# Attention followed by a mixer: the negated maxima reach their matrix row by a DMA instead of a masked multiplication

## The chip, the cores and the metric

The kernel runs on one core of a Trainium2 chip. A core has five engines that run in parallel, each through its own list of instructions in a fixed order: TensorE (PE; its weight loads are listed as PEld), VectorE (DVE), ScalarE (ACT), GpSimd (POOL) and SyncE (SP), which here issues all the DMAs. They wait for each other on semaphores. The metric is the device time of one execution in microseconds (us), lower is better; the number compared is the median of several runs.

## What is computed

```python
def _attn_ref(q, k, v):                     # 8 batches x 8 heads, 576 rows, 64 columns, float32
    scores = scale * np.matmul(q, k.transpose(0, 1, 3, 2))
    mask = block_i >= block_j               # blocks of 64 rows: causal by block
    scores = np.where(mask, scores, -1000000000.0)
    scores = scores - np.max(scores, axis=-1, keepdims=True)
    attn = np.exp(scores)
    attn = attn / (np.sum(attn, axis=-1, keepdims=True) + 1e-09)
    return np.matmul(attn, v)

def _moe_ref(x, U, V, w_ch1, w_ch2):        # x: the heads side by side, 8 x 576 x 512
    h = x.transpose(0, 2, 1) @ U @ V        # mixing over the rows, rank 32
    u = x + h.transpose(0, 2, 1)
    return u + np.maximum(u @ w_ch1, 0.0) @ w_ch2     # 512 -> 2048 -> 512
```

## The kernel before

There are 64 heads. For one head the work runs through these steps, each a function of the kernel that adds tasks to a list:

- `split_qk` fetches q and k (transposed, 64 x 1152) into `raw`, rounds them into `qa` and `kk`, and puts what the rounding lost into `qb` and the second half of `kk`. Two DMAs (`qb<-qa`, `kk<-kk`) copy rounded parts into other partitions. The subtractions that give the lost parts can run on POOL or on DVE.
- `maxima` multiplies queries by keys on PE (lines L1255 and L1257), takes the negated maximum of each row of scores on DVE (L1264, into five columns of `mx`), transposes these columns on PE (L1272) and copies the resulting 5 x 128 block to `mr` on ACT or DVE (L1276, L1277). Then `spread` (L1281, POOL or DVE) multiplies this block by `sel`, a 5 x 640 mask of ones and zeros, and writes 5 x 640 elements into rows 96 to 100 of `qa`. In each column only one of the five rows is not zero. The five rows of `kk` that meet them in the next product are ones, so that product adds the negated maximum of a query to all its scores.
- `probabilities` multiplies keys by queries (L1303 with `qa`, L1304 with `qb`), this time with the maxima in, and takes the exponential on ACT (L1317 for heads 0 to 7, L1325 after them) with a scale of 0.125 and, as a bias read from the tile `lift`, 8 ln 2. From head 8 on the result is split in two float16 parts `pp` (L1328 on ACT, L1333 on DVE).
- `apply_v` multiplies by the values (L1353, L1357 to L1359); `mix` does, after every second head, the mixing over rows (L1402, L1416, L1419).

Eight heads make a batch. When the eight are done, the feed-forward network can work on that batch, in chunks of 288 rows: `ffn_chunk` (first product L657, second L682) for the first half of the 2048 hidden columns. When all heads are done, `block_products` (L899) does the second half.

The order of all of this is not the order of the code. A planner, class `Plan`, keeps a table of tasks with an engine (or several to choose from), an estimated time, a priority (1000 x head for attention, from a million up for the feed-forward products) and dependencies. It plays these through, and whenever an engine is free in the plan it issues the ready task with the lowest priority number. Constants say when each engine starts (`START`), how long a result takes to be seen by another engine (`TAIL`, `INTO`), and how long a DMA lasts (`after=DL`, 3000 ns). PSUM banks come from pools: four in `banks_a` (of which `Rest` leaves one alone), one double bank in `banks_w`, two for the feed-forward in `banks_f`. In the plan's first 260 us, when PE has nothing to do, it issues a pair of matmuls of zeros (`idle`, L1503), counted as 225 ns.

Of the kernel before, what the change touches and what calls it, by code (L numbers as in the profile page):

```python
# [28 lines left out]
SCALE = 0.125  # L29
# [66 lines left out]
class Part:  # L96
# [8 lines left out]
    def __bool__(self):  # L105
        return bool(self._free())

    def pop(self, _):
        return self.pool.pop(self._free()[0])

    def append(self, x):
        self.pool.append(x)


class Rest:
# [175 lines left out]
def attention_then_mixer(  # L291
# [10 lines left out]
    nc = tc.nc  # L302
# [10 lines left out]
    def f32(ap):  # L313
        return ap.bitcast(F32)
# [734 lines left out]
    mx_r = [b.split(5) for b in ring(ap, 2, [P, P], F32, "mx")]  # L1049
    mr_r = ring(ap, 2, [P, P], F32, "mr")  # L1050
    sel = buf(ap, [P, 5, P], F32, "sel")
    vr_r = ring(ap, 2, [P, 10, D], F32, "vr")
# [22 lines left out]
    for n, fill in enumerate((1.0, NEG)):  # L1075
# [6 lines left out]
    make_identity(nc, ident.ap)  # L1082
    nc.gpsimd.memset(sel[96:P], 0.0)
    nc.gpsimd.affine_select(
        out=sel[96:P], in_=sel[96:P], pattern=[[-1, 5], [0, P]], compare_op=ALU.not_equal, fill=1.0, base=0,
        channel_multiplier=1,
    )
    nc.vector.memset(f32(qa_r[0][0:64, 0:64]), 0.0)
# [146 lines left out]
    def maxima(h, pr):  # L1235

        qa, kk, mx, mr = qa_r[h % NB], kk_r[h % NB], mx_r[h % 2], mr_r[h % 2]
        for tiles in ((4, 0), (3,), (2, 1)):
            wide = tiles[0] == 4
            bank = Buf(pool=banks_w if wide else Rest(banks_a))  # L1240
            parts, at = [], 0
            for i in tiles:
                n = P * i + 64
# [17 lines left out]
            for i, view in parts:  # L1261
# [6 lines left out]
                )  # L1268
        bank = Buf(pool=banks_a)
        rows = slice(96, 101)  # L1270
# [4 lines left out]
        add(  # L1275
            "ACT", _act(P), pr + 2, lambda: nc.scalar.copy(mr[rows], bank[rows, 0:P]), [bank], [mr],  # L1276
            others=[("DVE", _dve(P), lambda: nc.vector.tensor_copy(mr[rows], bank[rows, 0:P]), False, 50)],  # L1277
        )

        def spread(e):  # L1280
            return lambda: e.tensor_tensor(  # L1281
                out=qa[rows, :].rearrange("p (i c) -> p i c", i=5), in0=mr[rows].unsqueeze(1).to_broadcast([5, 5, P]),
                in1=sel[rows], op=ALU.mult,
            )

        add(
            "POOL", 1340, pr + 2, spread(nc.gpsimd), [mr], [qa.parts[1]], others=[("DVE", _dve(W), spread(nc.vector), True, 500)],
        )

    def probabilities(h, pr):  # L1290
# [5 lines left out]
        for g, (a, b, tiles) in enumerate(GROUPS):  # L1296
            bank = Buf(pool=Rest(banks_a) if g else banks_w)

# [11 lines left out]
            def shaped(x, g=g):  # L1310
                return x if g else x.rearrange("p (j k) -> p j k", j=2)

            view = lambda g=g, bank=bank, n=b - a: bank[:, :n] if g else bank[:, :, :320]
            if h < FW:
                add(
                    "ACT", _act(b - a) + 90, pr,
                    lambda view=view, at=at, shaped=shaped: nc.scalar.activation(  # L1317
                        shaped(pw_r[h % 2][:, at]), view(), AF.Exp, bias=lift[:, 0:1], scale=SCALE
                    ),
                    [bank], [ph.parts[g], pl.parts[g]],  # L1320
                )
                continue
            add(
                "ACT", _act(b - a) + 90, pr,
                lambda view=view: nc.scalar.activation(view(), view(), AF.Exp, bias=lift[:, 0:1], scale=SCALE), [], [bank],  # L1325
            )
# [10 lines left out]
    def apply_v(h, pr):  # L1337
# [40 lines left out]
    def mix(p, pr):  # L1378
# [166 lines left out]
```

## Time and profile before

| | us |
|---|---|
| median of three runs | 1136.38 |
| the three runs | 1133.79, 1136.38, 1136.84 |
| the profiled execution, whole | 1133.6 |
| its span, first to last instruction | 1131.5 |
| PE busy in the span | 1104.0 |
| DVE busy in the span | 973.8 |
| ACT busy in the span | 673.9 |
| POOL busy in the span | 443.7 |

The profile is of one execution. An engine is busy while one of its compute instructions runs. Idle time is listed with the instruction that followed it and with the engine whose result ended it. PE's matmuls of zeros count as busy although they compute nothing. Attention takes the part of the span up to about 630 us, with feed-forward products mixed in from batch to batch; what follows is feed-forward alone.

### The profile page before, as it was taken

Reading aid. Unit: us, or ns where it says so; the run is one execution under the profiler, and the core shown is the slowest. Engines: PE = TensorE matmul, PEld = TensorE weight load, DVE = VectorE, ACT = ScalarE, POOL = GpSimd, SP = SyncE. Lnnn points to the kernel's source line nnn. Section 1 sums busy time; section 2 is a strip of 40 time slices with the busy share of each in tenths; the row PEclk is TensorE's granted clock in tenths of the full one; section 3 lists DMA queues with packets and bytes.
Section 4 is the critical chain, followed back from the end, with each engine's and each line's share of the span. In section 5 each row is a group of like instructions: output and inputs, shape, how many; then the busy total and the mean of one; then the engine's idle time right before and its main releaser. Section 6 shows DMA issues by size and latency. Waiting matters only on the chain.

```text
span 1131.5 us, 27523 instructions
## 1 busy us (share of the span) xinstructions
PE 1104.0 (98%) x10722; PEld 921.2 (81%) x10722; DVE 973.8 (86%) x1983; ACT 673.9 (60%) x1294; POOL 443.7 (39%) x451
## 2 busy tenths in 40 slices
PE   9999998999999999999999999999999999999998
PEld 8897777888888888888888877777777777777776
DVE  7899899999999999999988537322799999999998
ACT  5568696777776778767767533531445545545543
POOL 4646565646586647564635293651000000000000
PEclk9999999999999999999999999999999999999999
DMA  7754565455455445445352225131231331340321
GB/s 166 190 154 119 173 190 138 139 137 147 132 148 141 131 127 147 127 117 140 98 127 54 72 68 163 43 85 48 59 103 35 116 116 35 102 127 32 95 85 42
DMA packets 82418, 126.39 MB, mean 112 GB/s; under 512 B 14448, under 2 KB 58480, under 8 KB 82288
## 3 DMA queue, kind: packets, MB, share of 16 engines
q1 hardware_dynamic: 82288, 124.64, 39.8%
q8 instruction: 84, 1.38, 0.5%
q14 instruction: 46, 0.38, 0.1%
HBM read 76.23 MB, written 29.49 MB: 93 GB/s over the span
## 4 chain that ended last, share of the span: by engine, by line
PE 61%; DVE 28%; ACT 4%; issue 3%; DMA 2%; POOL 2%; SPq 0%; POOLq 0%; DVEq 0%; ACTq 0%
PE bb L899 29%; DVE mx L1264 7%; PE bf L682 6%; PE bf L657 6%; PE bg L657 4%; PE bg L682 4%; DVE pp L1333 4%; DMA st<-in_w_dram 2%; DVE hl L665 1%; DVE wr L379 1%; DVE z L371 1%; PE ba L1357 1%; PE ba L1358 1%; PE ba L1359 1%; DVE x L1372 1%
## 5 line engine op out<-in xcount | busy, mean ns | idle before, releaser
L682 PEld LDWEIGHTS <-w2h 128*128 128x128 f16 x1024 | 100.3, 98 | 27.9 <-issue 2.6
L657 PEld LDWEIGHTS <-w1h 128*128 128x128 f16 x1024 | 97.7, 98 | 27.4 <-issue 3.0
L899 PE MATMUL bb<-hh,w1h 128*128 128x288 f16 x448 | 118.9, 286 | 0.0
L899 PE MATMUL bb<-hh,w1l 128*128 128x288 f16 x448 | 118.9, 286 | 0.0
L899 PE MATMUL bb<-hh,w2h 128*128 128x288 f16 x448 | 118.9, 286 | 0.0
L899 PE MATMUL bb<-hh,w2l 128*128 128x288 f16 x448 | 118.9, 286 | 0.0
L682 PE MATMUL bf<-hh,w2h 128*128 128x288 f16 x384 | 110.5, 288 | 2.4 <-DVE hl L665 2.4
L682 PE MATMUL bf<-hl,w2h 128*128 128x288 f16 x384 | 109.8, 286 | 0.0
L682 PE MATMUL bf<-hh,w2l 128*128 128x288 f16 x384 | 109.8, 286 | 0.0
L899 PEld LDWEIGHTS <-w1h 128*128 128x128 f16 x896 | 87.7, 98 | 21.9
L899 PEld LDWEIGHTS <-w2h 128*128 128x128 f16 x896 | 87.7, 98 | 21.9
L827 ACT CAST hh<-hb 128x576 f16<-128x576 f32 x96 | 63.8, 666 | 68.4 <-DVE hb L853 45.8
L899 PE MATMUL bb<-hl,w1h 128*128 128x288 f16 x448 | 91.6, 286 | 0.0
L899 PE MATMUL bb<-hl,w2h 128*128 128x288 f16 x448 | 91.6, 286 | 0.0
L1169 POOL TENSOR_TENSOR qb<-raw,qa 64x576 fp32r<-64x576 f32 x50 | 70.9, 1418 | 48.5 <-ACT pp L1328 9.3
L1357 PE MATMUL ba<-vv,pp 128*128 128x65 f16 x840 | 88.0, 194 | 0.3
L1358 PE MATMUL ba<-vv,pp 128*128 128x64 f16 x840 | 87.7, 195 | 0.0
L1359 PE MATMUL ba<-vv,pp 128*128 128x65 f16 x840 | 87.0, 192 | 0.2 <-DVE pp L1333 0.2
L1264 DVE TENSOR_REDUCE mx<-ba 128x1 f32<-128x448 f32 (+2 forms) x192 | 85.8, 476 | 0.9 <-ACT wr L483 0.6
L1281 POOL TENSOR_TENSOR qa<-mr,sel 5x640 fp32r<-5x640 f32 x44 | 67.8, 1541 | 40.1 <-ACT mr L1276 15.5
L1357 PEld LDWEIGHTS <-pp 128*128 128x128 f16 x840 | 77.8, 96 | 2.8 <-issue 0.9
L1358 PEld LDWEIGHTS <-pp 128*128 128x128 f16 x840 | 78.3, 97 | 1.7 <-issue 0.4
(227 smaller groups left out, 3459.5 us busy)
## 6 DMA issues: line engine op xcount, KB each, us to landing
raw<-in_qk_dram SPq DMA_DIRECT2D x63, 288.0 KB, 3.8
st<-in_w_dram SPq DMA_DIRECT2D x32, 512.0 KB, 4.3
o_d<-ot SPq DMA_DIRECT2D x72, 144.0 KB, 1.8
qb<-qa SPq DMA_DIRECT2D x64, 144.0 KB, 2.8
kk<-kk SPq DMA_DIRECT2D x64, 144.0 KB, 3.1
ur<-u_d SPq DMA_DIRECT2D x64, 144.0 KB, 2.7
wr<-o_d SPq DMA_DIRECT2D x32, 288.0 KB, 3.2
vr<-in_v_dram SPq DMA_DIRECT2D x28, 320.0 KB, 3.2
```

Source lines behind the costliest of these rows:

```text
L371: return nc.vector.scalar_tensor_tensor(out=z, in0=upp, scalar=-(1 << 30), in1=z, op0=ALU.bitwise_and, op1=ALU.bitwise_or)
L657: nc.tensor.matmul(ps[:, :T], w()[wn][:, k, fs], m[k].ap, start=(i == 0), stop=(i == len(ops) - 1))
L682: nc.tensor.matmul(ps[:, :T], w()[wn][:, f, ms], hs[f][x].ap, start=(i == 0), stop=(i == len(ops) - 1))
L827: add("ACT", _act(2 * T, True), E, lambda: nc.scalar.copy(h.ap, x[0]()), [x[1]], [h])
L899: nc.tensor.matmul(bank[:, i, :T], x()[:, w(k)], p.ap[:, k, :], start=first and n == 0, stop=last and n == len(ops) - 1)
L1169: sub = lambda e, dst=dst, x=x, y=y: lambda: e.tensor_sub(dst, raw[:, x], f32(y))
L1264: lambda i=i, view=view: nc.vector.tensor_reduce(out=mx[:, 96 + i : 97 + i], in_=view(), op=ALU.max, axis=AX.XY if i == 4 else AX.X, negat ...
L1281: return lambda: e.tensor_tensor(out=qa[rows, :].rearrange("p (i c) -> p i c", i=5), in0=mr[rows].unsqueeze(1).to_broadcast([5, 5, P]), in ...
L1333: lambda at=at, view=view, shaped=shaped: nc.vector.tensor_sub(shaped(pl[:, at]), view(), shaped(ph[:, at])),
L1357: nc.tensor.matmul(bank[:, o : o + D + 1], ph[:, w], vv[:, y, 0 : D + 1], start=(j == 0), stop=False)
L1358: nc.tensor.matmul(bank[:, o : o + D], ph[:, w], vv[:, y, D + 1 : 2 * D + 1], start=False, stop=False)
L1359: nc.tensor.matmul(bank[:, o : o + D + 1], pl[:, w], vv[:, y, 0 : D + 1], start=False, stop=(j == i))
```

## The change

The five rows are replaced by one. The copy out of PSUM (now L1287 on ACT, L1288 on DVE) adds a constant, 8 ln 2 / 0.125, to the 5 x 128 block and rounds it; then a DMA issued by SP (L1293) writes the five rows of 128 one after another into the single row 96 of `qa`. Rows 97 to 100 keep the zeros that the masks put there. The planner counts the DMA as 650 ns on SP and 2000 ns (`MD`) until it has landed. The exponentials have no bias operand any more, and the planner counts 90 ns less for each. The tiles `lift` and `sel` and what fills them go. `Either` lets tasks of heads 0 to 9 take a bank of `banks_a` or of `banks_f`. In the plan PE starts at 5000 ns instead of zero and DVE at 5600 instead of 5200.

```diff
+MD = 2000
-START = {"DVE": 5200, "ACT": 2750, "POOL": 5500, "SP": 700}
+START = {"PE": 5000, "DVE": 5600, "ACT": 2750, "POOL": 5500, "SP": 700}
+SH = 10
+class Either:
+    def __init__(self, *pools):
+        self.pools, self.home = pools, {id(x): p for p, _ in pools for x in p}
+    def __bool__(self):
+        return any(len(p) > n for p, n in self.pools)
+    def pop(self, n):
+        return next(p for p, k in self.pools if len(p) > k).pop(n)
+    early = Either((banks_a, 0), (banks_f, 0))
...
-            bank = Buf(pool=banks_w if wide else Rest(banks_a))
+            bank = Buf(pool=banks_w if wide else early if h < SH else Rest(banks_a))
...
-            "ACT", _act(P), pr + 2, lambda: nc.scalar.copy(mr[rows], bank[rows, 0:P]), [bank], [mr],
+            "ACT", _act(P), pr + 2, lambda: nc.scalar.activation(mr[rows], bank[rows, 0:P], AF.Copy, bias=LIFT * LN2 / SCALE), [bank], [mr],
...
-        def spread(e):
-            return lambda: e.tensor_tensor(
-                out=qa[rows, :].rearrange("p (i c) -> p i c", i=5), in0=mr[rows].unsqueeze(1).to_broadcast([5, 5, P]),
-                in1=sel[rows], op=ALU.mult,
-            )
-            "POOL", 1340, pr + 2, spread(nc.gpsimd), [mr], [qa.parts[1]], others=[("DVE", _dve(W), spread(nc.vector), True, 500)],
+            "SP", 650, pr + 2,
+            lambda: nc.sync.dma_start(
+                out=f32(qa[96:97, :]), in_=f32(mr[rows, :]),
+            ),
+            [mr], [qa.parts[1]], after=MD,
...
-                "ACT", _act(b - a) + 90, pr,
-                lambda view=view: nc.scalar.activation(view(), view(), AF.Exp, bias=lift[:, 0:1], scale=SCALE), [], [bank],
+                "ACT", _act(b - a), pr,
+                lambda view=view: nc.scalar.activation(view(), view(), AF.Exp, scale=SCALE), [], [bank],
```

The same replacement of the pool is made in `probabilities`, `apply_v` and `mix`.

Since the planner is run anew with these numbers, the order on every engine changes. Three places matter below. The first is the start of PE's list: nine matmuls of zeros, then pairs of them (54 matmuls before, 10 now), then the first scores of head 0. The names are PSUM banks (`bf`, `bw`, `ba`) and the tiles named above. Before, its end reads:

```order
L1503 LDWEIGHTS zero
L1503 MATMUL bf_88<-zero 128x256
L1255 MATMUL bw<-kk_155,qa_152 128x288 x2
L1257 MATMUL bw<-kk_155,qa_152 128x64
L1257 MATMUL ba_92<-kk_155,qa_152 128x448
L1257 MATMUL ba_93<-kk_155,qa_152 128x320
L1257 MATMUL ba_93<-kk_155,qa_152 128x192
```

And now:

```order
L1512 LDWEIGHTS zero
L1512 MATMUL bf_88<-zero 128x256
L1266 MATMUL bw<-kk_153,qa_150 128x288 x2
L1268 MATMUL bw<-kk_153,qa_150 128x64
L1268 MATMUL ba_92<-kk_153,qa_150 128x448
L1268 MATMUL ba_93<-kk_153,qa_150 128x320
L1268 MATMUL ba_93<-kk_153,qa_150 128x192
```

The five score products of head 0 are the same; 44 matmuls of zeros that stood ahead of them are gone. In the whole list there are 372 matmuls of 128 x 256 zeros before and 238 now.

The second place is DVE's list after the set-up of the masks (`marks`), where the maxima of head 0 (into `mx`) are taken; `z` and `st` belong to the weights. Before:

```order
L1096 CAST kk_155<-marks 64x640
L1169 TENSOR_TENSOR qb_158<-raw_150,qa_152 64x576
L1169 TENSOR_TENSOR kk_155<-raw_150,kk_155 64x576
L1264 TENSOR_REDUCE mx_165<-bw 128x1 x2
L1264 TENSOR_REDUCE mx_165<-ba_92 128x1
L1264 TENSOR_REDUCE mx_165<-ba_93 128x1 x2
L366 TENSOR_SCALAR z_99<-z_99 128x128
L1111 CAST qa_154<-marks 64x640
L371 SCALAR_TENSOR_TENSOR z_99<-st_97,z_99 128x128
L1111 CAST kk_157<-marks 64x640
L1169 TENSOR_TENSOR qb_159<-raw_151,qa_153 64x576
L1281 TENSOR_TENSOR qa_152<-mr_167,sel 5x640
```

And now:

```order
L1107 CAST kk_153<-marks 64x640
L1275 TENSOR_REDUCE mx_163<-bw 128x1 x2
L1275 TENSOR_REDUCE mx_163<-ba_92 128x1
L1275 TENSOR_REDUCE mx_163<-ba_93 128x1 x2
L1122 CAST kk_154<-marks 64x640
L385 TENSOR_SCALAR z_99<-z_99 128x128
L390 SCALAR_TENSOR_TENSOR z_99<-st_97,z_99 128x128
L1174 CAST qa_151<-raw_149 64x576
L398 SCALAR_TENSOR_TENSOR z_99<-st_97,z_99 128x128
L1180 TENSOR_TENSOR qb_157<-raw_149,qa_151 64x576
```

The two subtractions of head 0 have moved to POOL, so the maxima come right after the masks, and the spread of head 0 (the last row of before) has left DVE. Over the whole list DVE loses all of its 20 spreads, five of its 12 subtractions into `xl`, three of eight into `vv`, two of 22 into `kk` and two of four into `w1l`; POOL loses its 44 spreads and takes those subtractions.

The third place is SP's list, where the new DMA of head 0 stands. Before:

```order
L1154 DMA raw_150<-in_qk_dram 64x1152
L1188 DMA vr_171<-in_v_dram 128x640
L1174 DMA qb_159<-qa_153 64x576
L1174 DMA kk_156<-kk_156 64x576
L1174 DMA qb_160<-qa_154 64x576
L1138 DMA st_97<-in_V_dram 32x576 x3
```

And now:

```order
L1165 DMA raw_148<-in_qk_dram 64x1152
L1185 DMA qb_157<-qa_151 64x576
L1293 DMA qa_150<-mr_165 1x5x128
L1185 DMA kk_154<-kk_154 64x576
L1149 DMA st_97<-in_V_dram 32x576 x3
L1165 DMA raw_149<-in_qk_dram 64x1152
```

The DMA of head 0's maxima stands behind a DMA of head 1, and in front of another one of head 1, of three loads for the mixing and of the fetch of a later head. There are 64 such DMAs in the list, 609 DMAs in all instead of 545.

## Rows read from the trace of the kernel before

**Rows 1.** The page, parts 1 and 2: span, engines, granted TensorE clock.

```profile
span 1131.5 us, 27523 instructions
...
PE 1104.0 (98%) x10722; PEld 921.2 (81%) x10722; DVE 973.8 (86%) x1983; ACT 673.9 (60%) x1294; POOL 443.7 (39%) x451
...
DVE  7899899999999999999988537322799999999998
...
PEclk9999999999999999999999999999999999999999
```

**Rows 2.** Busy time of each engine in four stretches (the header names the columns).

```profile
core 0: us, PE busy (x) PEld busy (x) DVE busy (x) ACT busy (x) POOL busy (x), PEclk, DMA share, GB/s
0.00:100.00 100.00, 93.91 (x785) 85.62 (x786) 88.56 (x213) 59.46 (x122) 51.51 (x68) 0.98 0.66 165
100.00:260.00 160.00, 151.60 (x1659) 128.10 (x1658) 154.01 (x359) 123.04 (x249) 93.12 (x91) 1.00 0.53 148
260.00:640.00 380.00, 370.22 (x4309) 318.62 (x4306) 351.76 (x822) 271.58 (x570) 219.74 (x220) 1.00 0.46 123
640.00:1131.00 491.00, 488.24 (x3980) 388.86 (x3978) 379.49 (x592) 219.82 (x357) 79.34 (x74) 1.00 0.27 80
```

**Rows 3.** The same view for L1503 alone, the matmuls of zeros.

```profile
0.00:11.00 11.00, 6.06 (x54) 5.29 (x54) 1.00 0.90 193
11.00:100.00 89.00, 22.85 (x168) 15.34 (x168) 0.98 0.63 162
100.00:260.00 160.00, 19.43 (x152) 13.86 (x150) 1.00 0.53 148
```

**Rows 4.** Timeline of the start: start, length in us, engine, line.

```profile
4.37 0.67 ACT L1162 CAST kk<-raw 64x576 fp32r<-64x576 f32 x1
...
4.56 6.06 PE L1503 MATMUL bf<-zero 128*128 128x256 f16 x54
...
5.09 0.57 DVE L1096 CAST kk<-marks 64x640 fp32r<-64x640 f32 x1
...
10.38 0.51 PE L1255 MATMUL bw<-kk,qa 96*128 96x288 f32 x2
...
10.96 0.89 DVE L1264 TENSOR_REDUCE mx<-bw 128x1 f32<-128x576 f32 x2 [3.29 <-PE bw L1257]
...
15.35 0.82 DVE L1281 TENSOR_TENSOR qa<-mr,sel 5x640 fp32r<-5x640 f32 x1
...
16.23 0.47 PE L1303 MATMUL ba<-qa,kk 128*128 128x448 f32 x1 [0.34 <-DVE qa L1281]
```

**Rows 5.** Groups of instructions by line: busy us, mean ns of one, idle before.

```profile
L1281 POOL TENSOR_TENSOR qa<-mr,sel 5x640 fp32r<-5x640 f32 x44 | 67.8, 1541 | 40.1 <-ACT mr L1276 15.5 <-DVE mr L1277 5.6 <-DVE z L371 5.2
...
L1325 ACT ACTIVATE ba<-ba,lift 128x512 f32<-128x512 f32 x56 | 36.7, 656 | 5.3 <-PE ba L1304 3.8 <-DVE rv L1367 1.4
...
L1328 ACT CAST pp<-ba 128x512 f16<-128x512 f32 x56 | 33.3, 594 | 0.2
...
L1281 DVE TENSOR_TENSOR qa<-mr,sel 5x640 fp32r<-5x640 f32 x20 | 19.8, 989 | 0.6
```

**Rows 6.** Waits of PE: us in total, times, longest.

```profile
PE bw L1303 <- POOL qa L1281: 1.4, 3, 0.6
...
PE ba L1303 <- POOL qa L1281: 0.9, 3, 0.5
...
PE ba L1303 <- DVE qa L1281: 0.3, 1, 0.3
...
PE ba L1303 <- DMA u_d<-ut: 0.2, 1, 0.2
```

**Rows 7.** DMA issues: count, KB each, median us to landing.

```profile
o_d<-ot SPq DMA_DIRECT2D x72, 144.0 KB, 1.8
...
kk<-kk SPq DMA_DIRECT2D x64, 144.0 KB, 3.1
...
st<-in_V_dram SPq DMA_DIRECT2D x6, 72.0 KB, 2.0
```

More of the change, by code (lines that the diff above doesn't have):

```diff
@@ L128, in append @@
         self.pool.append(x)
+class Either:
[5 more added lines that the diff above has]
+        return next(p for p, k in self.pools if len(p) > k).pop(n)
+    def append(self, x):
+        self.home[id(x)].append(x)
 ENGINES = ("DVE", "PE", "ACT", "POOL", "SP")
@@ L1049, in attention_then_mixer @@
     mx_r = [b.split(5) for b in ring(ap, 2, [P, P], F32, "mx")]
[L1050 to L1051 removed]
+    mr_r = ring(ap, 2, [P, P], F32R, "mr")
     vr_r = ring(ap, 2, [P, 10, D], F32, "vr")
@@ L1082, in attention_then_mixer @@
     make_identity(nc, ident.ap)
[L1083 to L1086, printed above, removed]
-    )
     nc.vector.memset(f32(qa_r[0][0:64, 0:64]), 0.0)
@@ L1268, in maxima @@
                 )
-        bank = Buf(pool=banks_a)
+        bank = Buf(pool=early if h < SH else banks_a)
         rows = slice(96, 101)
@@ L1275, in maxima @@
         add(
-            "ACT", _act(P), pr + 2, lambda: nc.scalar.copy(mr[rows], bank[rows, 0:P]), [bank], [mr],
-            others=[("DVE", _dve(P), lambda: nc.vector.tensor_copy(mr[rows], bank[rows, 0:P]), False, 50)],
-        )
-        def spread(e):
-            return lambda: e.tensor_tensor(
-                out=qa[rows, :].rearrange("p (i c) -> p i c", i=5), in0=mr[rows].unsqueeze(1).to_broadcast([5, 5, P]),
-                in1=sel[rows], op=ALU.mult,
-            )
-        add(
-            "POOL", 1340, pr + 2, spread(nc.gpsimd), [mr], [qa.parts[1]], others=[("DVE", _dve(W), spread(nc.vector), True, 500)],
+            "ACT", _act(P), pr + 2, lambda: nc.scalar.activation(mr[rows], bank[rows, 0:P], AF.Copy, bias=LIFT * LN2 / SCALE), [bank], [mr],
+            others=[("DVE", _dve(P), lambda: nc.vector.tensor_scalar_add(mr[rows], bank[rows, 0:P], LIFT * LN2 / SCALE), False, 50)],
+        )
+        add(
+            "SP", 650, pr + 2,
[3 more added lines that the diff above has]
+            [mr], [qa.parts[1]], after=MD,
         )
@@ L1296, in probabilities @@
         for g, (a, b, tiles) in enumerate(GROUPS):
-            bank = Buf(pool=Rest(banks_a) if g else banks_w)
+            bank = Buf(pool=(early if h < SH else Rest(banks_a)) if g else banks_w)
             def products(g=g, tiles=tiles, bank=bank):
@@ L1315, in probabilities @@
                 add(
-                    "ACT", _act(b - a) + 90, pr,
+                    "ACT", _act(b - a), pr,
                     lambda view=view, at=at, shaped=shaped: nc.scalar.activation(
-                        shaped(pw_r[h % 2][:, at]), view(), AF.Exp, bias=lift[:, 0:1], scale=SCALE
+                        shaped(pw_r[h % 2][:, at]), view(), AF.Exp, scale=SCALE
                     ),
@@ L1323, in probabilities @@
             add(
-                "ACT", _act(b - a) + 90, pr,
-                lambda view=view: nc.scalar.activation(view(), view(), AF.Exp, bias=lift[:, 0:1], scale=SCALE), [], [bank],
+                "ACT", _act(b - a), pr,
+                lambda view=view: nc.scalar.activation(view(), view(), AF.Exp, scale=SCALE), [], [bank],
             )
@@ L1342, in apply_v @@
         xb = x.parts[s]
-        bank = Buf(pool=banks_a)
+        bank = Buf(pool=early if h < SH else banks_a)
         view = lambda: bank[:, : 5 * (D + 1)].rearrange("p (i c) -> p i c", i=5)
@@ L1395, in mix @@
         )
-        bank = Buf(pool=banks_a)
+        bank = Buf(pool=early if 2 * p < SH else banks_a)
         lows = bank
@@ L1411, in mix @@
         for g, (js, a, n) in enumerate((((0, 1, 2), 0, 384), ((3, 4), 384, 192))):
-            bank = Buf(pool=banks_a)
+            bank = Buf(pool=early if 2 * p < SH else banks_a)
             def products(bank=bank, js=js, a=a, n=n):
```

2 lines of the change are left out of this document (removed).

## The prediction

> **What bounds the kernel now.** I read the page's first two parts, then the table of stretches, and then looked for work on the busiest engine that isn't work. PE is busy for 1104.0 of 1131.5 us, DVE for 973.8; DVE's slices stand at nine tenths until about 560 us and then fall, and the granted clock of TensorE stands at nine tenths or more of 2.4 GHz in every slice [rows 1]. The stretches say the same in numbers [rows 2]: after 640 us PE has 488.2 busy of 491, so only the amount of its work counts there. From 260 to 640 us it has 370.2 of 380, because feed-forward products of finished batches fill what attention leaves. Before that it looks as full (93.9 of 100, 151.6 of 160), but here the matmuls of zeros are counted in: 6.06 us of them up to 11 us, 22.85 up to 100, 19.43 up to 260 [rows 3], 48.3 us together. They are issued where the plan has nothing for PE. So in the first 260 us it is the chain through the other engines that decides, and there DVE has 88.6 of 100 and 154.0 of 160 us [rows 2].
>
> PE's real work is 1104.0 − 48.3 = 1055.7 us, and the change takes nothing from it but the zeros. What can be won is therefore in the rest of the span, 1131.5 − 1055.7 = 75.8 us: 48.3 of zeros and 27.5 of idling (by stretch 6.1, 8.4, 9.8 and 3.2 [rows 2]). Anything that only makes attention end earlier after 260 us is given back: then fewer feed-forward products lie inside attention and more come behind it. The order says that this will happen: when PE reaches the 64th transposition of maxima it has issued 1686 feed-forward products before and 1506 now. I give those 180 no price, since PE has to run them in either place.
>
> **The start.** PE's first scores wait for the rounded keys of head 0 (ACT, 4.37 + 0.67 = 5.04 us) and for the masks (DVE, 5.09 + 0.57 = 5.66 us), but run at 10.38, without idle time before them, at the end of 54 matmuls of zeros that began at 4.56 and take 6.06 us [rows 4]. That queue, and no data, held them back. DVE sat idle for 3.29 us until they came [rows 4]. The plan lets PE begin at its zero with pairs of zeros, while on the chip they begin only behind the nine matmuls of the set-up; the new start time of 5000 leaves 10 of the 54. They take 10 x 6.06/54 = 1.1 us and end at 4.56 + 1.1 = 5.7 us, when the masks are there too. So the chain begins at about 5.8 instead of 10.38 us: **−4.6 us**. DVE's two subtractions ahead of the maxima go to POOL, so they don't eat this. It is certain as far as PE's first products go; what would take it back is a first product of probabilities (16.23 us before, released by DVE's spread that started at 15.35 [rows 4]) that now waits for its DMA.
>
> **Fewer gaps in the plan.** Beside the first block there are 318 matmuls of zeros before and 238 − 10 = 228 now. The 318 took 22.85 + 19.43 = 42.3 us [rows 3], 0.133 us each, so 90 fewer are **−12.0 us**. That is a price for PE time that the plan no longer needs to fill. It is a gain only if what made the plan shorter is real on the chip, so here is what stands behind it. DVE loses 20 spreads (19.8 us) and POOL 44 (67.8 us, 1541 ns each [rows 5]), and the order gives POOL a dozen subtractions that DVE had. ACT loses the bias operand in 192 exponentials: one of 512 columns takes 656 ns against 594 for a plain copy of the same size from the same place [rows 5], so at most about 62 ns each, 12 us in all, while the plan takes 90 ns each. ACT is the least certain of these, and also the least needed: it has 59.5 of 100 and 123.0 of 160 us [rows 2]. The two extra banks let a third product of an early head start without waiting for an exponential; they cost nothing, since no feed-forward product stands in the list before the tenth transposition, neither before nor now. Below, the term is bounded by nothing (every zero comes back as waiting) and by twice its size (the remaining 24.3 us of idling before 640 us shrink by half as well).
>
> **The new hop.** Before, a head's maxima went from `mr` to `qa` in 1541 ns on POOL or 989 on DVE, plus the queue of that engine. PE lost 1.4 + 0.9 + 0.3 = 2.6 us in seven waits for it [rows 6]. That goes: −2.6 us. Now 64 DMAs of 2.5 KB do it. The trace has none so small. From below: the quickest kinds, 144 KB into DRAM and 72 KB from it, land after 1.8 and 2.0 us; from above: the copies of keys between partitions, 144 KB, land after 3.1 us in the median [rows 7]. The plan allows 0.65 + 2.0 = 2.65 us. With 2.0 us nothing is late and the term is 0; with 3.1 us each of 64 heads is 0.45 late, 29 us if PE had nothing to run meanwhile. In the list SP holds the first new DMA behind one of head 1 (`qb`), which waits for a rounded copy; behind it stand that head's `kk`, the loads for the mixing and the fetch of a later head, so a late `mr` now delays them too, and PE waits for those a head later. I take 5 us, nearer to the lower end, because PE lost only 0.2 us to any DMA while attention ran, with 128 copies of this kind [rows 6], although those are issued a head ahead and the new ones are not. Net of the waits that go: **+2.4 us**.
>
> A row and a rule meet here. The median of 72 KB is 2.0 us, that of 144 KB from SBUF to DRAM 1.8 [rows 7]: the size does not decide. The Trainium skill, page "DMA: Bandwidth & Descriptors", section "Rules for kernel authors", says to coalesce many small transfers, since below 64 KB one pays mostly overhead; the trace agrees with the part that it can show, as half the bytes are no quicker. By that rule these 64 DMAs are the wrong tool for 2.5 KB, and the time would be that of the third rival below, whose price comes from the rows alone.
>
> **Sum.** −4.6 − 12.0 + 2.4 = −14.2 us on an execution of 1133.6 us, whose span is 1131.5. That execution was at the quick end of the runs shown (1133.8 to 1136.8, median 1136.4), so for the median I take 1136.4 − 14.2 = 1122.2, about **1122 us**.
>
> **Rivals.**
> 1. The idling goes as well. DVE and POOL are freer than the plan's shape needs, so half of the 24.3 us of waits before 640 us goes with the zeros: 1122 − 12 = 1110 us. For it: many of those waits end on DVE or POOL. Against it: the plan fills what these engines win with other tasks, and DVE stays near its limit.
> 2. The zeros come back as waiting. If the early heads are held by something that the change leaves alone (loads of weights share DVE and the DMA queue; DMA share 0.66 in the first 100 us [rows 2]), PE waits where it ran zeros, and only the start and the hop are left: 1136.4 − 4.6 + 2.4 = 1134 us, and 1139 if the start is lost too. Against it: the spread that DVE and POOL lose stood in exactly this chain.
> 3. The DMA is late, and the kernel is slower. The mechanism: the plan puts a head's probability products where it thinks the DMA has landed, PE keeps its order, and each later landing stops it. The gain without the hop is 4.6 + 12.0 + 2.6 = 19.2 us; over 64 heads it is used up at 0.30 us a head. At the 0.45 us of the keys' median the time is 1136.4 − 19.2 + 29 = 1146 us. For it: those keys are copied through the same queue; against it: 2.5 KB are five rows, not 64, and other products usually stand ahead of the awaited one.
>
> **Chances and range.** The forecast 0.62 (1115 to 1129, by the ends of the hop short of the third rival), the first rival 0.16, the second 0.11, the third 0.11. Of this kernel a difference of 0.3%, 3.4 us, can be told from none, so faster means below 1133. The forecast and the first rival are faster (0.78), and of the second a half, 0.06: 0.84. The other half of it and a little of the third are within 0.3%: 0.07. Slower: 0.09. For eight in ten I go from 1109 (the first rival) to 1135 (the milder form of the second).
>
> **What would show it.** In the changed kernel's profile the first scores start near 5.8 us and the first product of probabilities near 11 to 12; the matmuls of zeros take about 31 us; POOL's busy time falls by some 50 us and DVE's by 20 to 30; an exponential of 512 columns takes about 600 ns; PE's waits for the new DMA add up to less than 10 us and its landing median lies between 1.8 and 2.7 us. After 640 us PE is as full as before. The prediction is wrong if PE's idle time outside the zeros grows by more than 10 us (then the rest of that table says whether the DMA or DVE ended it), or if its granted clock falls in a stretch where zeros were taken out.

## The result, and the profile after

The changed kernel takes 1118.45 us (median of 6 runs, 1113.65 to 1137.09), the kernel before 1133.59 us (6 runs on the same chip). The ratio is 0.9846, with a 95% interval of 0.9824 to 0.9868: faster by 1.5%, about 17 us at that ratio. The run of 1137.09 us, whose granted clock was 0.943, is left out of the ratio. The forecast was 1122 us; the sign and, roughly, the size came out, but several of the steps that led there did not.

The profiled execution took 1117.0 us. Its page, span, engines and granted clock (before: [rows 1]):

```profile
span 1115.2 us, 27334 instructions
...
PE 1090.7 (98%) x10588; PEld 912.4 (82%) x10588; DVE 936.7 (84%) x1946; ACT 655.2 (59%) x1294; POOL 389.9 (35%) x421
...
PEclk9998999999999999999999999999999999999999
```

Of the 16.3 us by which the span is shorter, PE's busy time gives 13.3 and its idle time 3.0 (27.5 before, 24.5 now). Four stretches, with the columns of [rows 2]:

```profile
0.00:100.00 100.00, 88.43 (x691) 80.79 (x692) 87.70 (x227) 65.09 (x135) 42.80 (x61) 0.96 0.72 181
100.00:260.00 160.00, 156.20 (x1783) 133.75 (x1780) 149.53 (x364) 122.43 (x258) 86.76 (x91) 0.98 0.57 155
260.00:640.00 380.00, 374.06 (x4274) 321.59 (x4273) 326.80 (x783) 258.24 (x563) 209.28 (x214) 1.00 0.45 122
640.00:1115.00 475.00, 471.97 (x3851) 376.30 (x3848) 372.64 (x575) 209.47 (x341) 51.04 (x56) 1.00 0.26 78
```

PE's idle time is 100 − 88.43 = 11.6 us in the first stretch, 3.8 in the second and 5.9 in the third, where it was 6.1, 8.4 and 9.8 us. So there is more idle time at the start, and less from 100 to 640 us. From 260 to 640 us DVE has 326.8 busy, not 351.8. The matmuls of zeros, which now stand on L1512 (as in [rows 3], stretches 0 to 11, 11 to 100, 100 to 260 us):

```profile
0.00:11.00 11.00, 5.23 (x40) 4.11 (x40) 1.00 0.87 178
11.00:100.00 89.00, 15.02 (x104) 10.13 (x104) 0.95 0.70 181
100.00:260.00 160.00, 12.57 (x94) 8.50 (x94) 0.98 0.57 155
```

They take 32.8 us, not 48.3. In the first 100 us they take 20.2 us instead of 28.9, so that PE's other work there is 88.4 − 20.2 = 68.2 us, against 93.9 − 28.9 = 65.0 before: in spite of its idle time the start is not behind. The 15.5 us that went are almost the whole gain, if they count as gain. The rest of PE's busy time is 1090.7 − 32.8 = 1057.9 us, 2.2 more than before: the same 10588 − 238 = 10350 matmuls at a slightly lower mean clock. Timeline of the start (start and length in us; a bracket gives the idle time before and its releaser; before: [rows 4]):

```profile
5.05 1.67 PE L1512 MATMUL bf<-zero 128*128 128x256 f16 x10
...
6.47 0.51 PE L1266 MATMUL bw<-kk,qa 96*128 96x288 f32 x2
...
7.05 0.89 DVE L1275 TENSOR_REDUCE mx<-bw 128x1 f32<-128x576 f32 x2 [1.40 <-PE bw L1268]
...
10.48 0.27 ACT L1287 ACTIVATE mr<-ba 5x128 fp32r<-5x128 f32 x1
...
11.19 0.82 SPq L1293 DMA_DIRECT2D qa<-mr  x1
...
14.98 0.38 PE L1312 MATMUL bw<-qa,kk 128*128 128x320 f32 x1 [0.77 <-DMA qa<-mr]
```

The first scores start at 6.47 us, not at 10.38. But the first product of probabilities starts at 14.98, only 1.25 us earlier than before, because it waits for the first new DMA: issued at 11.19, it landed 3.66 us later. (A landing is here the time from the start of SP's issue to the last of the copy's six semaphore updates in the trace.) The groups by line (busy us, mean ns of one), to be held against [rows 5]:

```profile
L1334 ACT ACTIVATE ba<-ba 128x512 f32<-128x512 f32 x55 | 32.1, 583 | 6.6 <-PE ba L1313 6.1 <-ACT hh L681 0.2
```

An exponential of 512 columns that goes back into its bank takes 583 ns, not 656. Those of heads 0 to 7, which write into `pp`, before and after:

```profile
L1317 ACT ACTIVATE pp<-ba,lift 128x512 f32<-128x512 f32 x8 | 5.5, 688 | 0.0
```

```profile
L1326 ACT ACTIVATE pp<-ba 128x512 f32<-128x512 f32 x8 | 4.8, 598 | 0.0
```

PE's longest waits (total us, times, longest; before: [rows 6]):

```profile
PE bw L1312 <- DMA qa<-mr: 2.5, 2, 1.8
PE bw L1312 <- DVE pp L1342: 2.4, 2, 1.9
PE ba L1312 <- DMA qa<-mr: 2.4, 2, 1.6
PE ba L1425 <- ACT wr L502: 1.6, 1, 1.6
PE ba L1425 <- ACT ur L1435: 1.5, 1, 1.5
PE bf L1312 <- DMA qa<-mr: 1.1, 1, 1.1
```

PE waited for the new DMA five times, 2.5 + 2.4 + 1.1 = 6.0 us in all. Where the long waits lie is shown by PE's timeline (first products behind them), in three cuttings:

```profile
29.35 0.44 PE L1312 MATMUL ba<-qa,kk 128*128 128x448 f32 x1 [1.58 <-DMA qa<-mr]
```

```profile
91.68 0.55 PE L1425 MATMUL ba<-ident,x 128*128 128x128 f32 x3 [1.57 <-ACT wr L502]
...
93.90 0.44 PE L1425 MATMUL ba<-ident,x 128*128 128x128 f32 x2 [1.50 <-ACT ur L1435]
...
96.31 0.63 PE L1312 MATMUL bw<-qa,kk 128*128 128x320 f32 x1 [1.88 <-DVE pp L1342]
```

```profile
213.67 0.38 PE L1312 MATMUL bw<-qa,kk 128*128 128x320 f32 x1 [1.77 <-DMA qa<-mr]
```

And this is the granted clock there, in stretches of 2 us (busy time of PE, PEld, DVE, ACT, POOL, then PEclk, DMA share, GB/s):

```profile
28.00:30.00 2.00, 0.65 (x3) 0.64 (x4) 0.36 (x2) 0.66 (x1) 0.61 (x1) 0.94 1.06 288
30.00:32.00 2.00, 2.00 (x10) 1.80 (x9) 2.00 (x6) 1.91 (x5) 0.00 (x0) 0.50 1.11 139
32.00:34.00 2.00, 2.00 (x15) 1.55 (x14) 2.00 (x5) 0.40 (x1) 1.06 (x2) 0.70 1.11 182
90.00:92.00 2.00, 0.43 (x6) 0.32 (x4) 1.93 (x4) 1.98 (x4) 0.53 (x1) 1.00 0.34 76
92.00:94.00 2.00, 0.50 (x5) 0.25 (x3) 0.73 (x2) 1.98 (x6) 1.74 (x2) 1.00 0.01 1
94.00:96.00 2.00, 0.43 (x3) 0.26 (x3) 1.97 (x4) 2.00 (x6) 0.47 (x1) 0.66 0.22 74
96.00:98.00 2.00, 1.69 (x8) 1.63 (x9) 1.87 (x6) 1.97 (x6) 0.93 (x1) 0.50 0.63 170
98.00:100.00 2.00, 2.00 (x21) 1.10 (x20) 1.16 (x6) 2.00 (x4) 0.00 (x0) 0.50 0.42 166
100.00:102.00 2.00, 2.00 (x38) 1.93 (x35) 1.35 (x3) 1.41 (x3) 1.50 (x2) 0.64 0.28 61
212.00:214.00 2.00, 0.33 (x2) 0.36 (x3) 2.00 (x7) 0.00 (x0) 0.61 (x1) 1.00 0.87 195
214.00:216.00 2.00, 2.00 (x13) 1.93 (x11) 1.48 (x3) 0.74 (x2) 0.50 (x1) 0.52 0.97 281
216.00:218.00 2.00, 2.00 (x11) 1.91 (x10) 0.72 (x2) 1.78 (x5) 0.00 (x0) 0.62 0.56 213
```

Behind each of the three places the clock stands at or near 0.50, the lower of its two levels (1.2 GHz), while PE has work again. What a stretch lacks in clock, times 2 us, is (0.06 + 0.50 + 0.30) x 2 = 1.7 us at the first place, (0.34 + 0.50 + 0.50 + 0.36) x 2 = 3.4 at the second and (0.48 + 0.38) x 2 = 1.7 at the third, 6.8 us together. Over the span, a mean clock of 0.994 is (1 − 0.994) x 1115 = 6.7 us, so these three are all of it; before it was 0.002 x 1131.5 = 2.3 us. Half of the 6.8 us follows a wait for the new DMA. Not every idle time of this length is followed by the lower level. In the trace of the kernel before, PE was idle for 2.45 us up to 196.12 us, and the clock stayed at 1.00:

```profile
196.12 0.41 PE L1303 MATMUL bw<-qa,kk 128*128 128x320 f32 x1 [2.45 <-DVE pp L1333]
```

```profile
196.00:198.00 2.00, 1.88 (x42) 1.88 (x43) 1.93 (x7) 2.00 (x3) 0.80 (x1) 1.00 0.29 96
```

### The profile page after: what moved, and what is told of

Its sections match the earlier page's. It is cut to its first block, busy times and chain, and to the rows that moved or that the text cites. A ratio compares the mean times of both kernels' runs of the same rounds, so it can differ in the third digit from the quotient of the medians.

```text
span 1115.2 us, 27334 instructions
## 1 busy us (share of the span) xinstructions
PE 1090.7 (98%) x10588; PEld 912.4 (82%) x10588; DVE 936.7 (84%) x1946; ACT 655.2 (59%) x1294; POOL 389.9 (35%) x421
## 4 chain that ended last, share of the span: by engine, by line
PE 59%; DVE 15%; ACT 6%; issue 2%; DMA 2%; POOL 0%; SPq 0%; DVEq 0%; POOLq 0%; ACTq 0%
PE bb L918 30%; PE bf L676 5%; PE bf L701 5%; PE bg L701 5%; PE bg L676 5%; DVE mx L1275 3%; DVE pp L1342 3%; ACT pp L1337 1%; ACT ba L1334 1%; PE ba L1312 1%; PE ba L1366 1%; PE ba L1367 1%; DVE x L1381 1%; PE ba L1368 1%; PE bw L1312 1%
## 5 line engine op out<-in xcount | busy, mean ns | idle before, releaser
L701 PE MATMUL bf<-hh,w2h 128*128 128x288 f16 x352 | 101.3, 288 | 0.1
L701 PE MATMUL bf<-hl,w2h 128*128 128x288 f16 x352 | 100.7, 286 | 0.0
L701 PE MATMUL bf<-hh,w2l 128*128 128x288 f16 x352 | 100.6, 286 | 0.0
L1180 POOL TENSOR_TENSOR qb<-raw,qa 64x576 fp32r<-64x576 f32 x50 | 70.4, 1409 | 79.7 <-ACT qa L1173 18.8
L1366 PE MATMUL ba<-vv,pp 128*128 128x65 f16 x825 | 85.6, 193 | 0.6 <-DVE mx L1275 0.4
L1367 PE MATMUL ba<-vv,pp 128*128 128x64 f16 x825 | 85.3, 195 | 0.0
L1368 PE MATMUL ba<-vv,pp 128*128 128x65 f16 x825 | 84.7, 191 | 0.2 <-DVE pp L1342 0.2
L1366 PEld LDWEIGHTS <-pp 128*128 128x128 f16 x840 | 77.9, 96 | 3.1 <-issue 1.5
L1367 PEld LDWEIGHTS <-pp 128*128 128x128 f16 x840 | 78.5, 97 | 1.6 <-issue 0.5
L1368 PEld LDWEIGHTS <-pp 128*128 128x128 f16 x840 | 78.5, 100 | 0.4 <-DVE pp L1342 0.4
```

The lines of the kernel that those rows point to most:

```text
L701: nc.tensor.matmul(ps[:, :T], w()[wn][:, f, ms], hs[f][x].ap, start=(i == 0), stop=(i == len(ops) - 1))
L1180: sub = lambda e, dst=dst, x=x, y=y: lambda: e.tensor_sub(dst, raw[:, x], f32(y))
L1366: nc.tensor.matmul(bank[:, o : o + D + 1], ph[:, w], vv[:, y, 0 : D + 1], start=(j == 0), stop=False)
L1367: nc.tensor.matmul(bank[:, o : o + D], ph[:, w], vv[:, y, D + 1 : 2 * D + 1], start=False, stop=False)
L1368: nc.tensor.matmul(bank[:, o : o + D + 1], pl[:, w], vv[:, y, 0 : D + 1], start=False, stop=(j == i))
```

## The experiments

The theory was the prediction's: a plan with fewer gaps is worth what its zeros took, and all parts of the change help to it. Rivals: that one part makes the whole gain, the zeros being no measure of it; and that the masked multiplication matters by its place in the chain, not by the time that it takes on POOL and DVE. "Idle" is PE's, from the span and its busy time in each profile. Kernel 3 is the one of experiment 3, and so on; zeros are the matmuls of zeros.

**1. The start alone** (in the kernel before)

```diff
-START = {"DVE": 5200, "ACT": 2750, "POOL": 5500, "SP": 700}
+START = {"PE": 5000, "DVE": 5600, "ACT": 2750, "POOL": 5500, "SP": 700}
```

> The kernel before with the new start times alone (PE 5000, DVE 5600). Its list has 294 matmuls of zeros instead of 372; the block ahead of the first scores has 10 instead of 54. The prediction's theory: first scores at 5.8 to 6.5 us instead of 10.4, worth 4 to 5 us, and 34 fewer zeros elsewhere at 0.133 us, 4.5 us: about 1125 to 1129 us against 1133.6. Rival (DVE and the loads hold the early heads anyway, so the head start is lost before the first batch is done): 1132 to 1134, with the lost zeros back as idle time.

Measured: 1132.45 us (12 runs, 1127.06 to 1135.62), ratio 0.9971 [0.9954, 0.9988]; 294 zeros instead of 372. The first scores start at 6.48 us, as in the changed kernel. The 12 runs go with their mean clock: at 1.000 and 0.995 the times were 1127.06 and 1128.03, at 0.989 they were 1134.97 and 1135.62. So an earlier start is worth some 6 us when the clock holds (a run of the kernel before at 1.000 took 1133.64). The profiled execution (1134.63 us, 0.991) has a clock of 0.90 over the first 100 us, which is 10 us lost there; that the other slower executions lose theirs at the same place is likely and not shown.

**2. The exponentials without bias operand alone**

```diff
-            "ACT", _act(P), pr + 2, lambda: nc.scalar.copy(mr[rows], bank[rows, 0:P]), [bank], [mr],
+            "ACT", _act(P), pr + 2, lambda: nc.scalar.activation(mr[rows], bank[rows, 0:P], AF.Copy, bias=LIFT * LN2 / SCALE), [bank], [mr],
...
-                "ACT", _act(b - a) + 90, pr,
-                lambda view=view: nc.scalar.activation(view(), view(), AF.Exp, bias=lift[:, 0:1], scale=SCALE), [], [bank],
+                "ACT", _act(b - a), pr,
+                lambda view=view: nc.scalar.activation(view(), view(), AF.Exp, scale=SCALE), [], [bank],
```

> The kernel before with the exponentials without bias operand alone (the constant goes into the copy of the maxima). 362 zeros instead of 372. Both theories: an exponential of 512 columns falls from 656 to about 600 ns, ACT's busy time by 10 to 13 us, the time by 0 to 3 us (1130.5 to 1133.6), since ACT has slack. More than 5 us would say that ACT's exponentials were on the path.

Measured: 1130.98 us (6 runs), 0.9957 [0.9943, 0.9972]: 4.9 us, more than I gave it. One exponential of 512 columns takes 580 ns. ACT is not the bound in any stretch, but PE's idle time still fell from 27.5 to 24.5 us.

**3. The DMA in place of the masked multiplication alone**

```diff
-            "POOL", 1340, pr + 2, spread(nc.gpsimd), [mr], [qa.parts[1]], others=[("DVE", _dve(W), spread(nc.vector), True, 500)],
+            "SP", 650, pr + 2,
+            lambda: nc.sync.dma_start(
+                out=f32(qa[96:97, :]), in_=f32(mr[rows, :]),
+            ),
+            [mr], [qa.parts[1]], after=MD,
```

> The kernel before with the DMA in place of the spread alone (bias kept in the exponentials, old start times, old banks). 352 zeros instead of 372. The prediction's theory (the spreads that DVE and POOL lose stood in the early chain): most of the 12 us of zeros less 2.4 us of new waits, 1123 to 1127 us. Rival (the gain is from the banks and the start; the DMA only swaps one hop for a longer one): 20 zeros x 0.133 = 2.7 us less, 2 to 6 us of waits for the DMA more, 1131 to 1137 us.

Measured: 1119.7 us (4 runs), 0.986 [0.9842, 0.9878]: 15.9 us, nearly the whole change and more than I gave it. From its page, its groups by line and the third stretch:

```profile
PE 1097.3 (98%) x10702; PEld 919.1 (82%) x10702; DVE 957.7 (86%) x1984; ACT 659.4 (59%) x1274; POOL 368.8 (33%) x406
```

```profile
L1502 PE MATMUL bf<-zero 128*128 128x256 f16 x352 | 47.8, 278 | 0.2
```

```profile
260.00:640.00 380.00, 374.33 (x4355) 323.98 (x4353) 336.23 (x808) 257.15 (x549) 174.63 (x196) 1.00 0.45 121
```

There are only 20 zeros fewer than before, and their time is 47.8 us, 0.5 less. The gain of 14.6 us in the span is elsewhere: idle 19.6 us, and 1097.3 − 47.8 = 1049.5 us of other work instead of 1055.7. The matmuls behind those 1049.5 us are the same 10702 − 352 = 10350 as before, and they did not become quicker: their own durations, with overlaps counted twice, add up to 2740.7 us in both traces. They overlap more. A matmul's end is modelled, so part of a wait can count as busy; what kept them apart before is not settled here. From 260 to 640 us PE is idle for 5.7 us, not 9.8. And among PE's waits in this trace there is none for the new DMA.

Where the gain arises can be estimated from the two traces without the split into busy and idle. Every matmul but the zeros is given the median distance from its start to the next one, as its kind has it in the trace of the kernel before; the time that has passed, less these costs, is lost time. Before, 63.7 us are lost by 260 us, 76.5 by 640 us and 80.8 at the end; here 57.4, 62.2 and 66.3. So some 6 us of the gain arise before 260 us, some 8 from there to 640 us, and next to nothing after that.

**4. The lent banks alone**

```diff
+    early = Either((banks_a, 0), (banks_f, 0))
...
-            bank = Buf(pool=banks_w if wide else Rest(banks_a))
+            bank = Buf(pool=banks_w if wide else early if h < SH else Rest(banks_a))
...
-        bank = Buf(pool=banks_a)
+        bank = Buf(pool=early if h < SH else banks_a)
```

> The kernel before with the two feed-forward banks lent to heads 0 to 9 alone. 290 zeros instead of 372. The prediction's theory gave the banks no price: 1132 to 1135 us. Rival (an early head is held by waiting for a free bank, and this is where most of the gain is): 82 zeros x 0.133 = 10.9 us, 1121 to 1125 us.

Measured: 1148.67 us (6 runs), 1.011 [1.0093, 1.0127]: slower by 12.5 us. The zeros by line, and the first two stretches:

```profile
L1521 PE MATMUL bf<-zero 128*128 128x256 f16 x290 | 39.1, 281 | 0.1
```

```profile
0.00:100.00 100.00, 90.61 (x662) 84.85 (x663) 82.90 (x195) 57.89 (x117) 52.94 (x67) 0.90 0.59 149
100.00:260.00 160.00, 145.37 (x1583) 120.86 (x1580) 152.69 (x362) 120.97 (x242) 90.04 (x87) 0.98 0.56 155
```

82 zeros fewer, 9.2 us of them, and the kernel is slower. PE is idle for 9.4 and 14.6 us where it was 6.1 and 8.4, and the clock is 0.90 in the first 100 us. Over the span it is 0.988 instead of 0.998, which is 11.5 us of 1146: the clock, too, is a large part of what the lent banks cost here. Taken by themselves, the zeros are no price.

**5. The changed kernel with the masked multiplication back**

```diff
-            "SP", 650, pr + 2,
-            lambda: nc.sync.dma_start(
-                out=f32(qa[96:97, :]), in_=f32(mr[rows, :]),
-            ),
-            [mr], [qa.parts[1]], after=MD,
+            "POOL", 1340, pr + 2, spread(nc.gpsimd), [mr], [qa.parts[1]], others=[("DVE", _dve(W), spread(nc.vector), True, 500)],
```

> The changed kernel with the masked multiplication back in place of the DMA (everything else as changed). 262 zeros instead of 238. The prediction's theory: the spreads come back on POOL and DVE, 1126 to 1130 us. Rival (the DMA is worth little): 24 zeros x 0.133 = 3.2 us more, and 6 us of PE's waits for the DMA and the dips of TensorE's clock behind them gone: 1112 to 1119 us, with a granted clock of 0.997 or more.

Measured: 1135.11 us (11 runs), 0.9999 [0.999, 1.0009]. Start, bias and banks together bring nothing without the DMA, although this kernel has 262 zeros, 110 fewer than before. From 260 to 640 us PE is idle for 10.5 us. By the estimate of kernel 3, 59.7, 75.0 and 79.3 us are lost by 260 us, by 640 us and at the end, against 52.8, 60.6 and 64.6 in the changed kernel: the DMA's effect is split over the stretches as in kernel 3.

**6. The changed kernel without lent banks**

```diff
-SH = 10
+SH = 0
```

> The changed kernel without the lent banks. 312 zeros instead of 238. The prediction's theory (banks cost and bring nothing): 1116 to 1120 us. Rival (banks are most of the gain): 74 zeros x 0.133 = 9.8 us more, 1125 to 1130 us.

Measured: 1114.72 us (4 runs, 1114.15 to 1115.58), 0.9826 [0.9813, 0.9839]. The interval overlaps the changed kernel's, so that the banks cost something there too is likely and not shown; what is plain is that the runs lie closer together, all at clocks of 0.998 to 1.0. 312 zeros, 74 more than the changed kernel, and not slower.

**7. Another order of the same work**

```diff
-VARIANT = 12
+VARIANT = 13
```

> The changed kernel with VARIANT 13 instead of 12: the planner's estimates are jittered by other numbers within 2%, nothing else differs. 294 zeros instead of 238. If a zero less in the plan is a gain on the chip: 56 x 0.133 = 7.4 us more, 1122 to 1128 us. If the number of zeros only says how the plan looked: 1115 to 1120 us. Either way this measures how much of the 15 us is the luck of one schedule.

Measured: 1124.07 us (6 runs), 0.9924 [0.9905, 0.9943]. `VARIANT` shifts the planner's time estimates by other amounts, each within 2%, and nothing else. That alone costs 0.8% of the 1.5%. The result lies where a price for each zero would have put it (1122 to 1128 us), so it does not speak against such a price; kernels 4 and 5 do. Single parts of a few us cannot be told from the accident of one order by one kernel each; the 15 us of the DMA can, since they show in two pairs (3 against before, the changed kernel against 5).

**8. A longer landing time in the plan**

```diff
-MD = 2000
+MD = 3500
```

> The changed kernel with the planner told that the DMA lands after 3500 ns instead of 2000. 246 zeros instead of 238. If late landings cost what PE's waits for the DMA show (6 us, and a share of the 6 us of low clock behind such gaps): PE's waits for the DMA below 2 us and 1110 to 1116 us. If the plan then only puts the products later: 1117 to 1122 us.

Measured: 1114.51 us (4 runs), 0.9823 [0.9805, 0.9841], against 0.9846 for 2000: intervals that overlap. Among PE's waits there is none for a DMA any more, and the mean clock of the profile is 0.997, not 0.994, though two of the other three runs have 0.991. The zeros are 246.

**9. and 10. The DMA, and the multiplication still done beside it** (kernel 3 with a dead multiplication into a tile that nobody reads, at the same priority; in 9 it may run on POOL or DVE, in 10 on POOL alone)

```diff
+        junk = junk_r[h % 2]
...
+                out=junk[rows, :].rearrange("p (i c) -> p i c", i=5), in0=f32(mr[rows]).unsqueeze(1).to_broadcast([5, 5, P]),
+                in1=sel[rows], op=ALU.mult,
...
+            "POOL", 1340, pr + 2, spread(nc.gpsimd), [mr], [junk], others=[("DVE", _dve(W), spread(nc.vector), True, 500)],
```

In 10 the last line ends behind `[junk],`.

> x_dma (the DMA alone, 0.986 of before) with the masked multiplication kept as dead work: POOL or DVE still does it for every head, at the same priority, into a tile that nobody reads, while the DMA feeds the products. 434 zeros. Theory (what the DMA saves is the time of POOL and DVE): the gain goes, 1129 to 1137 us, and PE's idle time from 260 to 640 us is back at about 10 us. Rival (the place of the spread in the chain from the maxima to the products was the cost, not its load): 1118 to 1123 us.

> As d_spread, but the dead multiplication runs on POOL alone, 64 of them, 99 us; DVE is free of it. 408 zeros. If DVE's time is the scarce one: near x_dma, 1119 to 1125 us. If POOL's time and its fixed order are (subtractions of the next heads wait behind the multiplication, which waits for the maxima): as slow as d_spread or slower, 1129 to 1140 us.

Measured: 1135.31 us (11 runs), 1.0006 [0.9996, 1.0016], and 1135.26 us (12 runs), 1.0007 [0.9995, 1.0018]. Both give back the whole gain of kernel 3. The dead multiplications by line, of 9 and then of 10, and 10's engines:

```profile
L1293 POOL TENSOR_TENSOR junk<-mr,sel 5x640 fp32r<-5x640 f32 x37 | 57.7, 1561 | 32.6 <-ACT pp L1340 7.0 <-DVE z L372 5.3 <-ACT mr L1278 5.2
...
L1293 DVE TENSOR_TENSOR junk<-mr,sel 5x640 fp32r<-5x640 f32 x27 | 23.4, 871 | 0.8
```

```profile
L1293 POOL TENSOR_TENSOR junk<-mr,sel 5x640 fp32r<-5x640 f32 x64 | 100.2, 1568 | 45.7 <-DVE z L380 10.2 <-ACT mr L1278 8.9 <-DVE mr L1279 5.9
```

```profile
PE 1110.7 (98%) x10758; PEld 926.4 (81%) x10758; DVE 962.9 (85%) x1971; ACT 671.6 (59%) x1293; POOL 468.8 (41%) x464
```

Nobody waits for the result of these instructions, so it is not their place between `mr` and `qa` that the DMA saves, but the room that they take in the lists of POOL and DVE: their time, with the wait for `mr` in front of it. 10 says more: with 100.2 us of it on POOL and none on DVE, POOL is busy for 41% and DVE for 962.9 us, 11 less than before; and still all is lost. By the estimate of kernel 3, 73.6 us are lost by 260 us and 81.4 by 640 us, against 57.4 and 62.2 there, so most of the loss arises before 260 us; from 260 to 640 us PE is idle for only 6.0 us, where it is 9.2 in kernel 9. How POOL's load does this is open. POOL runs its queue in order, so that a subtraction of head n + 1 may stand behind it, and behind its wait for `mr`; and the planner keeps some of DVE's work apart from POOL's, so a fuller POOL also narrows DVE's choice. No run separates the two.

**11. Early loads held back** (kernel 6, with the fetches for heads 8 to 11 held until head 3 is done)

```diff
-            writes=[raw], after=DL,
+            [begun] if 2 * p < FW + 4 else [], writes=[raw], after=DL,
...
+    begun = Buf()
...
+        if h == 3:
+            begun.writers = [len(plan.tasks) - 1]
```

> u_banks (the changed kernel without the lent banks, 0.983 of before) with the two early fetches of values for heads 8 to 11, 320 KB each, held back until head 3 is done. 274 zeros instead of 312. If the landings of 3.7 to 5.1 us of the first DMAs of maxima come from transfers ahead of them in the queue: the first one lands below 2.5 us, PE's waits for the DMA fall from 5.4 to below 3 us, 1109 to 1114 us. If the delay is given back later in the early stage: 1113 to 1117 us.

Measured: 1120.36 us (4 runs), 0.9874 [0.9858, 0.9889]; kernel 6 has 0.9826. PE's waits for the new DMA, first of kernel 6 and then of this one:

```profile
PE bw L1312 <- DMA qa<-mr: 3.9, 2, 2.2
...
PE ba L1312 <- DMA qa<-mr: 1.5, 1, 1.5
```

```profile
PE bw L1312 <- DMA qa<-mr: 0.4, 2, 0.2
```

The first of the DMAs now lands after 1.88 us instead of 5.09, and PE waits 0.4 us for them instead of 5.4: that first landing was late because of the loads. (The third still takes 4.12 us, where kernel 6 has 4.21.) But the time did not follow: 5.4 us slower, by the two ratios. In the profiles, whose spans differ by 2.9 us, the kernel with held loads has 8.9 us of idle time from 260 to 640 us, 4.7 more than kernel 6. My expectation missed in size and sign; waits of PE that a trace lists are no more a price than zeros are.

**12. Both settings together**

```diff
-MD = 2000
+MD = 3500
...
-SH = 10
+SH = 0
```

> The changed kernel without the lent banks and with the planner told 3500 ns for the DMA: the two edits that each were as quick as the change or quicker (0.9826 and 0.9823). 302 zeros. If they add: no waits for the DMA, granted clock 0.998 or more, 1106 to 1112 us. If both only remove the same waits and dips: 1111 to 1116 us.

Measured: 1111.68 us (5 runs, 1110.89 to 1116.23), 0.9806 [0.979, 0.9822]: 22.0 us below the kernel before, with an interval that ends just below the changed kernel's. Its median is below those of kernels 6 and 8, but the intervals overlap, so that it is faster than each setting alone is not shown. Its engines and clock:

```profile
PE 1090.6 (98%) x10652; PEld 912.4 (82%) x10652; DVE 946.0 (85%) x1959; ACT 649.8 (59%) x1285; POOL 386.1 (35%) x417
...
PEclk9999999999999999999999999999999999999999
```

PE is idle for 18.6 us of 1109.2, with 302 zeros, 64 more than the changed kernel has.

Taken together, the seven kernels that have the DMA and no masked multiplication, in seven orders of the work, have medians from 1111.7 to 1124.1 us; the seven in which POOL or DVE still does the multiplication have 1131.0 to 1148.7.

## Why the prediction was right or wrong

**The total** was near (1122 against 1118.45; as differences, −14.2 forecast and about −17 measured, since the median that I started from, 1136.4, was 2.8 us above the one found here). That is in good part luck. The DMA, which I had priced at +2.4 us and otherwise counted only as one cause of fewer zeros, gave nearly the whole gain by itself (−15.9, kernel 3), and the other edits cancel: alone, start −3.3, bias −4.9, banks +12.5 us; together without the DMA 0.0 (kernel 5).

**The start, −4.6 us.** The step held for PE's first scores (6.47 us; "about 5.8") and failed for what follows from them: the thing that I named as able to take it back, a first product that waits for its DMA, came, with 14.98 us for the first product of probabilities where I had "near 11 to 12". Alone it was worth 3.3 us (1.4 to 5.2 by its interval), and on the whole its runs are the slower, the lower their clock.

**Fewer gaps in the plan, −12.0 us.** This is the step that failed; that its number fits is luck. The zeros fell as the order had shown, 48.3 to 32.8 us. But "a price for PE time that the plan no longer needs to fill" does not hold: −9.2 us of zeros went with +12.5 us (kernel 4), 110 fewer with 0.0 (kernel 5), −0.5 us with −15.9 (kernel 3). The mechanism of the second rival, zeros that come back as waiting, did occur, for start, bias and banks together. In this step's place stands the room that the masked multiplication took in the lists of POOL and DVE (kernels 9 and 10), which I had listed as one of the things behind the plan, beside the others; how it reaches PE stays open.

**The banks at nothing.** Wrong alone (+1.1%). I had looked only at whether feed-forward products need the banks; what the trace shows is PE idle for 14.6 us instead of 8.4 from 100 to 260 us, and a clock of 0.988. Why the order with lent banks has these gaps is open. In the whole change their cost is not shown (kernel 6).

**"Given back" after 260 us.** Wrong. I had excluded the stretch from 260 to 640 us because feed-forward products fill PE there. They did not fill it: by the estimate of kernel 3, 12.8 us were lost there before and 4.8 in kernel 3, about half of the DMA's gain, and the end kept it. Its idle time fell from 9.8 to 5.9 us here, to 5.7 in kernel 3 and 4.2 in kernel 6, and rose to 10.5 in kernel 5. The idle time alone is no measure, though: kernel 10 has 6.0 us of it and none of the gain, kernel 11 has 8.9 and most of it.

**The hop, +2.4 us.** Right in mechanism and size: the seven waits of 2.6 us went, 6.0 us of waiting for the DMA came, net +3.4. Not in the term were the 1.7 + 1.7 us of clock behind two of these waits. The landings have a median of 2.06 us (1.71 to 4.14), inside "1.8 to 2.7"; eleven land after more than 3 us, four of them among the first ten. The third rival, late by 0.30 us or more a head, would need 19 us of waits; 6.0 came. The Trainium skill, "DMA: Bandwidth & Descriptors", section "Rules for kernel authors", holds small transfers to be mostly overhead. The trace agrees on the overhead: 2.5 KB take 2.06 us in the median where 144 KB into DRAM took 1.8 [rows 7]. But SP pays for it, and of the engines that compute only PE, with its 6.0 us of waits, so the rule did not decide here.

**The bias, "at most about 62 ns".** 656 to 583 is 73 ns: the exponential is now quicker than the plain copy (594) that I took for its floor. That copy writes float16 into `pp`, the exponential back into its bank, so it was no floor. The Trainium skill, "ScalarE: Activation LUTs", section "What ACT_TABLE_LOAD costs", states about 93 ns for a pointer operand. The trace comes close to it where the exponential writes into `pp` (heads 0 to 7): 90 ns at 512 columns (688 to 598), 84 at 640 (792 to 708). Where it writes back into its bank, no shape shows more than 76 (768 to 692 at 640 columns, 602 to 526 at 448).

**POOL and DVE.** POOL's busy time fell by 53.8 us ("some 50"), DVE's by 37.1 ("20 to 30").

**The warning on the clock** came true, at three places. In two stretches where zeros were taken out the clock fell: to 0.96 from 0.98 up to 100 us, to 0.98 from 1.00 up to 260 us. By this sign of my own the working was wrong, although the total held. It took back 6.7 − 2.3 = 4.4 us, which no term of the sum had. Kernel 6's profile, without lent banks, has a mean clock of 1.0.

**The first rival**, idling that goes with the zeros, did not come: 3.0 us of PE's idle time went, not 12.

## What to carry to other kernels

Count what an engine does to fill a plan's gaps as neither cost nor gain: here fewer of these matmuls went with a slower kernel and more of them with the fastest one. And do not take work on an engine that looks half idle for free: a multiplication of 1.5 us a head on POOL (busy for 39%), or 1.0 us where DVE did it, was worth 1.4% of the time, and a DMA of 2.5 KB that lands after 2 us took its place at almost no cost. Try each part alone before shipping a bundle: one part of this one costs 1.1% by itself.

## What the runs showed of the hardware

- A copy of 5 x 512 B between partitions keeps SP for 0.66 to 0.82 us in the issue (median 0.74), the 144 KB copies of `qb` and `kk` for 0.50 and 0.53 in the median. It lands after 1.71 us at the least and 4.14 at the most, in kernel 6 after up to 5.32 us.
- The multiplication of 5 partitions x 640 takes POOL 1541 ns [rows 5], more than a subtraction of 64 x 576 (1409 and 1418 ns on L1180): few partitions don't make it quick.
- One idle time of PE of 1.58 or 1.77 us, after which it had work again, was followed by stretches at or near the lower clock level that cost 1.7 us; three of them close together by stretches that cost 3.4 us. Another, of 2.45 us in the kernel before, was followed by none.
- A bias read from a tile costs an exponential 73 to 76 ns where it writes back into its PSUM bank, and 84 to 90 ns where it writes into `pp`.
